# Loading x a second time in 32x32 blocks, so that VectorE and not TensorE turns it

## The chip, the cores and the metric

The kernel runs on one core of one Trainium2 chip. The metric is the device time of the whole program in microseconds; before the change it is 756.91 (median of 3 runs, 756.82 to 757.55). The engines are called as in the profile: PE is TensorE (PEld its weight loads), DVE is VectorE, ACT is ScalarE, POOL is GpSimd, SP is SyncE, which here only issues transfers.

## What is computed

There are 8 batches. In each, 8 heads hold 512 tokens of 64 numbers (x) and 32 state vectors of 64 numbers. Scores between the tokens and the states are normalised once over the states (for each token) and once over the tokens (for each state):

```python
scores = scale * x @ state.T              # B,H,512,32
a   = softmax(scores);  xread = a  @ state
a2  = softmax(scale * state @ x.T);  sread = a2 @ x
y = concatenate([xread, sread], axis=2)   # 544 rows in each batch
y = y.transpose(0, 2, 1, 3).reshape(B * 544, 512)
h = y @ w_in                              # 512 -> 2048
g = where(h > 0, h, exp(min(h, 0)) - 1)
out = g @ w_out                           # 2048 -> 512
```

All of it is in float32.

## The kernel before

**Tiling.** x of a batch lies in memory as x_sb with tokens on the 128 partitions (four tokens each, r = 0 to 3) and the 8 heads times 64 numbers along the row. The scores need it the other way round, with the 64 numbers of a head on partitions, two heads (one "m") in 128: this turned copy is called xT, four pieces of 128x512 in two tiles. The state vectors stand turned in kT. The scores of all 8 heads fill two banks of PSUM, each with 4 heads x 32 states on partitions and 512 tokens along the row.

**The attention's output is never written out.** make_m multiplies the state vectors by w_in to m (128x512, for each quarter c of the 2048 columns), so that ffn1, h = aT x m, goes straight from the normalised scores aT to the hidden layer: for each of 16 column blocks fo a product in two steps, in a bank of PSUM, then elu: two ScalarE operations and one VectorE operation that writes g_all. ffn1 uses three banks in turn.

**The second product** (g_all x w_out) is done by Strassen's scheme, in a class of that name: sums of parts of g_all are made on VectorE, and its seven partial products are queued as a list of steps. The first four steps are two pieces each of the products p1 and p2; from batch 2 on, four of the products are themselves done in this manner (class Second). After each step one of a list of hooks is called, and these hooks are the attention of the next batch:

- s0 turns x of the next batch: turn_x puts 32 TensorE transposes (64x64 each) into PSUM, copy_x copies the result in four ScalarE operations to xT. These two tiles come from the pool "o".
- s1 does the scores, make_m for the column quarters 0 and 1, and most of the softmax on VectorE, ScalarE and GpSimd.
- s2 turns the weights over tokens (turn_state), the last hook reads the state update (state_read, from x_sb) and keeps it.

**Order.** TensorE and SyncE follow the order in which the program names their instructions (class InOrder). ScalarE and GpSimd are held to it in the first batch only, VectorE until the end of batch 1's ffn1; after that a planner orders each engine's instructions by its estimates and their place in the program. The first batch has an order written out by hand and keeps its own turn of x for batches 0 and 1.

**Buffers and transfers.** Pool "o" has two buffers of 128x2x512 for all tiles with that tag: the two halves of a batch's output (o_sb) and, before the change, the two xT tiles. Pool "work" has 11 of the same size, six of which hold weight sums from batch 1 on. SyncE's queue holds, in each batch: the two stores of the previous output, the fetch of two w_in parts that had to give up their place (fetch_w_in, called at fo 6), a second such fetch together with s1, and the load of x_sb two batches ahead.

Of the kernel before, what the change touches and what calls it, by code (L numbers as in the profile page):

```python
# [10 lines left out]
FP32 = mybir.dt.float32  # L11
# [14 lines left out]
def kernel(  # L26
# [15 lines left out]
    B, H, S, D = x.shape  # L42
    NS = state.shape[2]
    DM, DF = moe_w_in.shape
    P = 128
    R = S // P
# [18 lines left out]
    def pool(name, bufs, **kw):  # L65
        return ctx.enter_context(tc.tile_pool(name=name, bufs=bufs, **kw))
# [6 lines left out]
    work = pool("work", NRAW + 4)  # L73
    small = pool("small", 4)
    epool = pool("elu", 3)
    opool = pool("o", 2)
# [8 lines left out]
    def bank(i):  # L85
        return psum[:, i]

    def pair(i):

        return psum[:, i : i + 2]  # L90
# [3 lines left out]
    class InOrder:  # L94
# [10 lines left out]
    tensor, sync, vector, scalar, gpsimd = (  # L105
        InOrder(e) for e in (nc.tensor, nc.sync, nc.vector, nc.scalar, nc.gpsimd)
    )
    matmul = tensor.matmul

    def transpose(out, in_):  # L110


        for t in range(2):
            rows = slice(t * 64, (t + 1) * 64)
            tensor.transpose(out[:, t], in_[rows], ident[rows, rows], tile_position=(t * 64, 0))
# [15 lines left out]
    x_t, st, m_t = {}, {}, {}  # L131

    def load_x(b, engines):
        x_t[b] = xpool.tile([P, R, DM], FP32, name="x_sb")
        x_v = x[b].rearrange("h (p r) d -> p r h d", r=R)
        for r in range(R):
            engines[r % len(engines)].dma_start(
                out=x_t[b][:, r].rearrange("p (h d) -> p h d", d=D), in_=x_v[:, r]
            )

    state_v = state.rearrange("b (m c) n d -> c m n b d", c=G)

# [82 lines left out]
    def turn_x(b, i, first=6):  # L225

        ps = pair(first).rearrange("p t (j r q) -> p t j r q", j=2, q=64)
        for j in range(2):
            for r in range(R):
                m = 2 * i + j  # L230
                transpose(ps[:, :, j, r], x_t[b][:, r, m * P : (m + 1) * P])
        st[b, "xT", i] = ps

    def copy_x(b, i):
        xT = opool.tile([P, 2, R * P], FP32, tag="o", name="xT")
        for j in range(2):
            st[b, 2 * i + j] = xT[:, j]
            scalar.copy(
                out=xT[:, j].rearrange("p (r t q) -> p t r q", t=2, q=64),
                in_=st[b, "xT", i][:, :, j],  # L240
            )
# [19 lines left out]
    def scores(b):  # L261

        st[b, "s_ps"] = by_state(b, [st[b, m][:, None] for m in range(NP)])
# [57 lines left out]
    def turn_state(b):  # L321
        ps = st[b, "sT"] = pair(6).rearrange("p g (r q) -> p g r q", r=R)
        for g in range(G):
            a = st[b, g, "a_s"].rearrange("p (r q) -> p r q", r=R)
            for r in range(R):
                tensor.transpose(ps[:, g, r], a[:, r], ident)

    def copy_state(b):
        st[b, "aT_s"] = work.tile([P, G, R, P], FP32, tag="w", name="aT_s")
        for g in range(G):  # L330
            scalar.copy(out=st[b, "aT_s"][:, g], in_=st[b, "sT"][:, g])

    def state_read(b):


        ps = st[b, "sr"] = pair(6)
        for g in range(G):
            for r in range(R):
                for m in range(NP):
                    matmul(  # L340
                        ps[m * NS : (m + 1) * NS, g, :D],
                        st[b, "aT_s"][:, g, r, m * NS : (m + 1) * NS],
                        x_t[b][:, r, m * P + g * D : m * P + (g + 1) * D],
                        start=(r == 0),
                        stop=(r == R - 1),
                        tile_position=(0, m * NS),
                    )

    def keep_read(b):
        for g in range(G):  # L350
            scalar.activation(
                out=read[:, b, g], in_=st[b, "sr"][:, g, :D], func=AF.Copy,
                scale=st[b, g, "total"],
            )
# [14 lines left out]
    def fetch_w_in(c, k):  # L369

        for i in range(2):
            sync.dma_start(
                out=w_in[:, 2 * (k + i) : 2 * (k + i) + 2],
                in_=w_in_mem[:, 2 * (c + i) : 2 * (c + i) + 2],
            )

    def make_m(b, c, h=None, first=6):

        c_in = c if b < 2 else c % 2
        halves = slice(2 * c_in, 2 * c_in + 2) if h is None else slice(2 * c_in + h, 2 * c_in + h + 1)  # L380
        assert h is None or b == 0
        st[b, "m", c] = by_state(b, [w_in[:, halves, m] for m in range(NP)], first)

    def copy_m(b, c, g, copy):
        if g == 0:
            m_t[b, c] = mpool.tile([P, G, 512], FP32, name="m_sb")
        copy(out=m_t[b, c][:, g], in_=st[b, "m", c][:, g])
# [8 lines left out]
    def exp_part(ps):  # L396
        e = epool.tile([P, ps.shape[-1]], FP32, tag="e", name="e_sb")
        scalar.activation(out=e, in_=ps, func=AF.Relu, scale=-1.0)
        scalar.activation(out=e, in_=e, func=AF.Exp, scale=-1.0)
        return e  # L400

    def max_part(fo, e, ps):
        vector.scalar_tensor_tensor(
            out=g_all[:, fo, : ps.shape[-1]], in0=e, scalar=-1.0, in1=ps,
            op0=ALU.add, op1=ALU.max,
        )

    def elu(ps, fo):

        max_part(fo, exp_part(ps), ps)  # L410

    def ffn1(b, fo):


        ps = bank(4 + fo % 2 if b == 0 else 3 + (fo + 1) % 3)
        for k in range(G):
            matmul(
                ps,
                m_t[b, fo // 4][:, k, fo % 4 * P : (fo % 4 + 1) * P],
                st[b, k, "aT"],  # L420
                start=(k == 0),
                stop=(k == G - 1),
            )
        return ps
# [243 lines left out]
    def attention(b):  # L668


        def both(*fs):
            for g in range(G):
                for f in fs:
                    f(b, g)

        def s0():

            for i in range(2):
                turn_x(b, i, 4 + 2 * i)
            for i in range(2):  # L680
                copy_x(b, i)

        def s1():

            scores(b)
            for c in range(2):
                make_m(b, c, first=4 - 2 * c)
            both(column_max, turn_scores, column_exp, row_max, row_subtract, row_exp)
            both(row_sum, row_scale, column_total)
            for c in range(2):  # L690
                for g in range(G):
                    copy_m(b, c, g, (scalar.copy, vector.tensor_copy)[g])

        def s2():
            turn_state(b)
            copy_state(b)
            both(turn_tokens)

        nop = lambda: None
        return [s0, s1, nop, nop, s2, lambda: (state_read(b), keep_read(b))]  # L700

    def store(b, i, o_sb):
        rows = out_b[b, 0:S].rearrange("(p r) c -> p r c", r=R)
        sync.dma_start(out=rows[:, 2 * i : 2 * i + 2], in_=o_sb)
# [107 lines left out]
            store(0, i, o_sb)  # L812

    def batch(b):
        for fo in range(FO):
            elu(ffn1(b, fo), fo)
            if fo == FO // 4 + 1:
                for c in (2, 3):
                    make_m(b, c, first=6 if c == 2 else 0)
            if FO // 4 + 1 <= fo < FO // 4 + 5:  # L820
                c, g = divmod(fo - FO // 4 - 1, G)
                copy_m(b, 2 + c, g, vector.tensor_copy)
            if b == 1 and fo % 2 == 1:
                weight_sum((1, 2, 4, 3)[fo // 4], fo % 4 // 2)
            if b > 1 and fo == FO // 4 + 2:
                fetch_w_in(0, 0)
        vector.on = False
        nxt = b + 1 < B
        hooks = attention(b + 1) if nxt else [turn_read]
        if nxt and b > 0:  # L830
            s1 = hooks[1]
            hooks[1] = lambda: (s1(), fetch_w_in(2, 0))
        if b + 2 < B:
            hooks += [lambda: load_x(b + 2, [sync])]
        if b == 1:
            hooks += [lambda: second[4].weights(t_w[4]), lambda: second[3].weights(b22)]
            hooks += [lambda: second[5].weights(t_w[1]), lambda: second[7].weights(t_w[3])]
            used = {k: second[k] for k in (4, 3)}
        else:
            used = second  # L840
        whole = Strassen(2, used)
        whole.sums()
        for f in whole.steps():
            f()
            if hooks:
                hooks.pop(0)()
        if not nxt:
            fetch_w_in(2, 2)
        for i in (1, 0):
            store(b, i, whole.o_sb[i])  # L850
# [61 lines left out]
```

## Time and profile before

The profile shows one execution, 756.0 us long. A batch in the middle, from one turn to the next, has these times (the batch that turns x of batch 4, from the timeline; the next batch starts 82.07 us later with the same steps):

| What | From us | Length us |
|---|---|---|
| ffn1, 16 column blocks, with make_m for quarters 2 and 3 between | 295.6 | 29.5 |
| first piece of p1 | 325.10 | 3.6 |
| turn of x (TensorE) | 328.65 | 1.2 |
| second piece of p1 | 329.80 | 3.7 |
| scores, make_m for quarters 0 and 1 | 333.45 | 2.7 |
| p2 | 336.18 | 7.2 |
| first piece of the third product | 343.19 | 3.6 |
| state read | 351.07 | 1.1 |
| last output store issued (of the batch before) | 296.1 | 2.7 to landing |
| w_in fetch, two transfers of 1 MB | 307.17 | to about 314 |

Groups that concern the change, from the answers on the tiles x_sb and xT:

| Operation | Count | Median ns |
|---|---|---|
| PE MATMUL ps<-ident,x_sb (turns of x; half of the records carry a form) | 256 | 223 |
| PE MATMUL ps<-xT,kT (scores) | 128 | 613 |
| ACT COPY xT<-ps | 32 | 591 |
| transfers x_sb<-in_x_dram, 256 KB each | 32 | 4.5 us to landing |

How to read it: records of TensorE overlap, so the length of a step is read from the start of one to the start of the next. A number in brackets at the end of a row of the timeline is the idle time of that engine ahead of the instruction, with what ended it. Every instruction of the kernel carries line 100, since a helper records them all; groups are told apart by the names of their tiles.

### The profile page before, as it was taken

How to read it: one execution, taken by the hardware profiler on the slowest of the kernel's cores; microseconds unless marked ns; L12 is line 12 of the kernel's file. 1: busy time of each engine (PE TensorE's matmuls, PEld its weight loads, DVE VectorE, ACT ScalarE, POOL GpSimd, SP SyncE). 2: the span in 40 equal slices, each digit the busy share in tenths (PEclk: the TensorE clock that was granted, in tenths of full speed). 3: DMA queues.
4: the chain of work that ended last, by engine and by line, in shares of the span. 5: the costliest groups of instructions: out<-in, count | busy, mean ns of one | idle time of the engine just before them, and what ended most of it. 6: DMA issues, size and time to landing. Idle time of an engine off the chain costs nothing.

```text
span 756.0 us, 11509 instructions
## 1 busy us (share of the span) xinstructions
PE 736.2 (97%) x4712; PEld 512.6 (68%) x4712; DVE 465.4 (62%) x856; ACT 312.0 (41%) x575; POOL 34.4 (5%) x38
## 2 busy tenths in 40 slices
PE   4899999999999999999999999999999999999997
PEld 2544344368955797468946795479846894699886
DVE  2999974899246673667455763667366755557330
ACT  5899955653036311642055303631164205510420
POOL 0200002002000200011000200020000100000000
PEclk9999999999999999999999999999999999999999
DMA  9667900403212331214030221233121103003000
GB/s 284 212 202 245 310 0 23 91 1 117 51 64 104 112 57 57 111 69 100 29 140 0 113 56 60 108 113 56 57 112 57 56 29 139 1 0 141 28 4 26
DMA packets 49566, 66.81 MB, mean 88 GB/s; under 512 B 36968, under 2 KB 37480, under 8 KB 45672
## 3 DMA queue, kind: packets, MB, share of 16 engines
q1 hardware_dynamic: 47204, 65.45, 26.3%
q10 hardware_dynamic: 2308, 0.62, 0.4%
q8 instruction: 37, 0.61, 0.4%
q14 instruction: 17, 0.14, 0.1%
HBM read 52.95 MB, written 13.11 MB: 87 GB/s over the span
## 4 chain that ended last, share of the span: by engine, by line
PE 93%; DVE 3%; DMA 1%; ACT 1%; ACTq 0%; issue 0%; DVEq 0%
PE ps L100 93%; DVE w_in L100 1%; DMA x_sb<-in_x_dram 1%; DVE s L100 0%; DMA raw<-in_moe_w_out_dram 0%; DVE w_out L100 0%; ACT xT L100 0%; DVE g_all L100 0%; ACTq L100 0%; DVE top L100 0%; ACT raw L100 0%; ACT a_s L100 0%; DVE t_sb L100 0%; ACT e_sb L100 0%; DVE aT L100 0%; DVE m_sb L100 0%
## 5 line engine op out<-in xcount | busy, mean ns | idle before, releaser
L100 PE MATMUL ps<-w_out,g_all 128*128 128x256 f32 (+2 forms) x1088 | 234.8, 367 | 1.5 <-DVE g_all L100 0.8
L100 PE MATMUL ps<-aT,m_sb 128*128 128x512 f32 x512 | 226.3, 595 | 1.1 <-DVE m_sb L100 0.8
L100 PEld LDWEIGHTS ps<-w_out,g_all 128*128 128x128 f32 x1088 | 175.6, 191 | 55.0 <-issue 37.1
L100 PEld LDWEIGHTS ps<-aT,m_sb 128*128 128x128 f32 x512 | 95.4, 190 | 122.0 <-issue 116.9
L100 ACT ACTIVATE e_sb<-ps 128x512 f32<-128x512 f32 (+1 forms) x144 | 82.5, 573 | 218.8 <-PE ps L100 203.5
L100 DVE SCALAR_TENSOR_TENSOR g_all<-e_sb,ps 128x512 f32<-128x512 f32 (+1 forms) x144 | 94.4, 657 | 112.5 <-ACT e_sb L100 112.4
L100 DVE TENSOR_TENSOR o_sb<-o_sb,ps 128x128 f32<-128x128 f32 (+2 forms) x170 | 52.8, 310 | 76.1 <-PE ps L100 74.4
L100 PE MATMUL ps<-t_w,s 128*128 128x256 f32 (+1 forms) x480 | 89.3, 338 | 0.0
L100 ACT ACTIVATE e_sb<-e_sb 128x512 f32<-128x512 f32 (+1 forms) x144 | 87.3, 606 | 4.6
L100 PEld LDWEIGHTS ps<-t_w,s 128*128 128x128 f32 x480 | 77.1, 191 | 7.3 <-DVE o_sb L100 0.2
L100 ACT COPY o_sb<-ps 128x512 f32<-128x512 f32 (+2 forms) x52 | 21.2, 424 | 122.2 <-PE ps L100 115.2
L100 ACT ACTIVATE raw<-raw 128x512 f32<-128x512 uint32 x64 | 43.8, 684 | 1.0
L100 POOL TENSOR_TENSOR t_sb<-t_sb,top_t 128x512 f32<-128x512 f32 x16 | 16.7, 1049 | 533.5 <-DVE top_t L100 533.5
L100 DVE TENSOR_TENSOR s<-s,g_all 128x512 f32<-128x512 f32 (+1 forms) x36 | 32.1, 896 | 14.4 <-PE ps L100 14.2
L100 DVE TENSOR_TENSOR g_all<-g_all,s 128x512 f32<-128x512 f32 (+1 forms) x36 | 31.9, 886 | 9.6 <-PE ps L100 9.6
L100 PE MATMUL ps<-w_in,kT 64*32 64x512 f32 (+1 forms) x576 | 33.2, 547 | 0.8 <-ACT a_s L100 0.8
L100 DVE TENSOR_TENSOR g_all<-g_all 128x512 f32<-128x512 f32 (+1 forms) x36 | 32.2, 895 | 0.5
L100 PE MATMUL ps<-t_w,g_all 128*128 128x128 f32 (+1 forms) x240 | 32.1, 282 | 0.0
L100 DVE TENSOR_TENSOR s<-g_all 128x512 f32<-128x512 f32 (+1 forms) x36 | 31.6, 895 | 0.5
L100 PE MATMUL ps<-w_in,s 128*128 128x128 f32 x240 | 30.7, 275 | 0.0
L100 PEld LDWEIGHTS ps<-t_w,g_all 128*128 128x128 f32 x240 | 29.8, 192 | 0.5
L100 PEld LDWEIGHTS ps<-w_in,s 128*128 128x128 f32 x240 | 28.7, 192 | 0.0
(82 smaller groups left out, 574.8 us busy)
## 6 DMA issues: line engine op xcount, KB each, us to landing
w_in<-w_in_mem SPq DMA_DIRECT2D x26, 1024.0 KB, 5.9
raw<-in_moe_w_in_dram SPq DMA_DIRECT2D x16, 512.0 KB, 4.9
raw<-in_moe_w_out_dram SPq DMA_DIRECT2D x16, 512.0 KB, 4.4
out_dram<-o_sb SPq DMA_DIRECT2D x16, 512.0 KB, 2.6
x_sb<-in_x_dram SPq DMA_DIRECT2D x30, 256.0 KB, 4.5
w_in_mem<-w_in SPq DMA_DIRECT2D x4, 1024.0 KB, 8.6
x_sb<-in_x_dram ACTq DMA_DIRECT2D x2, 256.0 KB, 6.7
s_sb<-in_state_dram SPq DMA_DIRECT2D x8, 56.0 KB, 2.0
```

Source lines behind the costliest of these rows:

```text
L100: ins = getattr(self.engine, name)(*args, **kw)
```

## The change

x of batches 2 to 7 is loaded a second time. load_blocks, called at the start of the batch before, fetches it in pieces of 32 tokens by 32 numbers (128 bytes in a row), each placed where its turned counterpart belongs; what remains is to turn the inside of every 32x32 block. VectorE does so: turn_blocks, one 128x512 piece at each of fo 12 to 15. The raw blocks lie in pool "o" (before the output of that batch takes it), the turned ones in pool "work". TensorE's transposes and ScalarE's copies of these batches go, and with them s0; s1 moves up to the first hook, one piece of the product sooner, with a nop in its old place. It is meant to take the turn off TensorE. x_sb is still loaded, since state_read uses it.

```diff
+    def load_blocks(b):
+        for i in range(2):
+            st[b, "blocks", i] = raw = opool.tile([P, 2, R * P], FP32, tag="o", name="x_blocks")
+            for j in range(2):
+                for k in range(4):
+                    x_v = x[b, 2 * (2 * i + j) + k // 2].rearrange(
+                        "(q p r) d -> p r q d", q=P // 32, r=R
+                    )
+                    sync.dma_start(
+                        out=raw[k * 32 : (k + 1) * 32, j].rearrange(
+                            "p (r q d) -> p r q d", r=R, d=32
+                        ),
+                        in_=x_v[:, :, :, k % 2 * 32 : (k % 2 + 1) * 32],
+                    )
+
+    def turn_blocks(b, m):
+        i, j = divmod(m, 2)
+        if j == 0:
+            st[b, "xT", i] = work.tile([P, 2, R * P], FP32, tag="w", name="xT_b")
+        st[b, m] = st[b, "xT", i][:, j]
+        vector.transpose(st[b, m], st[b, "blocks", i][:, j])
...
-        def s0():
-            for i in range(2):
-                turn_x(b, i, 4 + 2 * i)
-            for i in range(2):
-                copy_x(b, i)
...
-        return [s0, s1, nop, nop, s2, lambda: (state_read(b), keep_read(b))]
+        return [s1, nop, nop, nop, s2, lambda: (state_read(b), keep_read(b))]
...
     def batch(b):
+        if b + 1 < B:
+            load_blocks(b + 1)
         for fo in range(FO):
             elu(ffn1(b, fo), fo)
+            if fo > 11 and b + 1 < B:
+                turn_blocks(b + 1, fo - 12)
...
-            s1 = hooks[1]
-            hooks[1] = lambda: (s1(), fetch_w_in(2, 0))
+            s1 = hooks[0]
+            hooks[0] = lambda: (s1(), fetch_w_in(2, 0))
```

## The prediction, as put on record before the result was known

> **What bounds the kernel now.** I read the busy times first, then the chain of waits in order of time, then the timeline of one middle batch. From the page:
>
> ```profile
> PE 736.2 (97%) x4712; PEld 512.6 (68%) x4712; DVE 465.4 (62%) x856; ACT 312.0 (41%) x575; POOL 34.4 (5%) x38
> PE 93%; DVE 3%; DMA 1%; ACT 1%; ACTq 0%; issue 0%; DVEq 0%
> ```
>
> TensorE (PE) is busy 97% of the span, and the chain that ended last is 93% TensorE. In order of time, its later part repeats (start, length, what):
>
> ```profile
> 273.12 81.05 PE ps L100 x560
> 354.17 0.04 DVEq L100
> 354.20 0.73 DVE s L100 x2
> 354.94 0.21 DVE o_sb L100
> 355.14 0.04 issue
> 355.19 81.05 PE ps L100 x560
> ```
>
> A batch lasts 82.07 us (355.19 less 273.12), 81.05 of them unbroken TensorE work. So in the middle batches, a microsecond taken out of TensorE's queue comes off the total, and one added to another engine costs nothing until TensorE waits for it. The timeline where the first Strassen product of batch 3 begins, while x of batch 4 is turned (start, length, engine, operation):
>
> ```profile
> 325.10 3.62 PE L100 MATMUL ps<-w_out,g_all 128*128 128x256 f32 x16
> ...
> 328.65 1.22 PE L100 MATMUL ps<-ident,x_sb 64*128 64x64 f32 x32
> ...
> 329.40 2.05 ACT L100 COPY xT<-ps 128x512 f32<-128x512 f32 x4 [2.84 <-PE ps L100]
> ...
> 329.80 3.72 PE L100 MATMUL ps<-w_out,g_all 128*128 128x256 f32 x16
> ...
> 333.45 1.09 PE L100 MATMUL ps<-xT,kT 64*32 64x512 f32 x16
> ...
> 336.18 7.17 PE L100 MATMUL ps<-w_out,g_all 128*128 128x256 f32 x32
> ```
>
> TensorE goes from one piece of the product to the 32 transposes, to the next piece, to the scores, with no idle time noted: starts follow one another. The four ScalarE copies run beside the second piece, so they are off the path.
>
> **What the skill says.** "VectorE: DVE Perf Modes", section "The three transpose paths": VectorE transposes only within 32x32 blocks, so blocks must be placed by something else; here the loads do it. The trace shows that operation at 0.71 us for 128x512 out of on-chip memory (line below). "DMA: Bandwidth & Descriptors", section "Specifications", names 512 B as the least size for full rate; the trace agrees: the 256 B pieces of x move at 216 to 289 GB/s, the 4 KB rows of the output at 401. The same page, "Why small descriptors are slow (HBM only)", gives a piece 3 cycles above its 32-byte beats: 11 for 256 B, hence 7 for 128 B. No run here shows 128 B pieces yet.
>
> **Removed from TensorE and ScalarE.** The turn stands from 328.65 to the next piece at 329.80: 1.15 us, on the path. Moving the scores forward one piece changes order, not work. From 325.10 to 336.18 there are 11.08 us; without the turn I count two pieces of 16 x 0.2235 (the spacing that 3.576 us for 16 gives), 7.15, and scores with make_m, 336.18 less 333.45, 2.73, and about 0.08 for changing to the tiled form, as between the second piece and the scores now: 9.96. That gives 1.12, near the 1.15. I take 1.13. Batches 1 to 6 do this for the next one: 6 x 1.13 = 6.8 us. Four ScalarE copies per batch (median 0.59 us) go too, at nothing gained, since the pieces hide them.
>
> **Added to VectorE.** Four block transposes per batch; the nearest row has the same shape:
>
> ```profile
> 342.38 0.71 DVE L100 STREAM_TRANSPOSE aT<-t_sb 128x512 f32<-128x512 f32 x1 [0.56 <-POOL t_sb L100]
> ```
>
> In ffn1, VectorE does one 0.69 us operation every 1.72 us and sits idle 1.03 us before it:
>
> ```profile
> 321.44 0.69 DVE L100 SCALAR_TENSOR_TENSOR g_all<-e_sb,ps 128x512 f32<-128x512 f32 x1 [1.03 <-ACT e_sb L100]
> ...
> 323.16 0.69 DVE L100 SCALAR_TENSOR_TENSOR g_all<-e_sb,ps 128x512 f32<-128x512 f32 x1 [1.03 <-ACT e_sb L100]
> ```
>
> Counting back from the last at 326.74, these belong to fo 12 and 13. A 0.71 us transpose fits into each gap, so 4 x 0.71 = 2.84 us per batch lie beside matmuls: cost nothing. The last, behind fo 15's elu (326.74 + 0.69), would end about 328.1, with scores due at 328.7. Batch 1 is tighter: VectorE runs almost without gaps from 149 to 169 us, as it also makes weight sums there. Turn 3 then follows the elu that ends at 162.2; with one 1.22 us sum ahead of it, it ends at 164.1, against scores due at 163.6. I charge 0 to 1 us once, and take 0.2.
>
> **Added to the loads.** 16 transfers per batch, each 32 partitions x 16 pieces of 128 B: 8192 pieces, 512 on each of 16 DMA engines, 1 MB. The nearest rows are those of the normal load of x (4096 pieces of 256 B), half-microsecond windows with clock, DMA share and GB/s:
>
> ```profile
> 354.00:354.50 0.50, 1.00 1.27 289
> 354.50:355.00 0.50, 1.00 1.19 267
> 355.00:355.50 0.50, 1.00 1.22 238
> 355.50:356.00 0.50, 1.00 1.31 228
> ```
>
> The eight windows from 354 to 358 average 240 GB/s, that is 256 B x 16 / 240 = 17 ns per piece on one engine. A 128 B piece costs, at best, 7/11 of that (the page's beats): 10.9 ns, 5.6 us per batch; at worst I allow twice the 256 B price, 34 ns, 17.4 us. I take the same 17 ns, 8.7 us. The transfers need the two o buffers, free once the output of the batch before has been stored; the second store is issued at 296.1 and its bytes end at about 298.4. So data from 298.4, the first tile complete half way at 302.8 and the second at 307.1, plus 1.9 us (the normal load's bulk ends at 358.0, its last landing at 354.1 + 5.8): 304.7 and 309.0. Behind them on SyncE's queue stands the w_in fetch, issued at 307.17 now and finished near 314; delayed to about 316, it still meets make_m at 329. In program order the first turn is due at 322.1: 17 us to spare, and 8 at the worst price. Cost: nothing.
>
> **Added waits.** A turn waits on a transfer; behind it on VectorE stand the elu of following fo, on which ffn1's three banks hang. This is where it can fail: only in batch 1's ffn1 is VectorE held to program order. Afterwards its order is the planner's, which puts an instruction into the first gap where it believes the data there (a 1.22 us sum for the product already stands at 311.87, between two elus). If it believes that the blocks land sooner than they do, VectorE stands still. The buffers for the turned x (work pool) are free during ffn1; the previous product's sums are done.
>
> Sum: 756.91 - 6.8 + 0.2 = 750.3 us.
>
> **Rivals.**
> (A) All hidden, 750.3. For it: the gaps and the spare time above.
> (B) Turns placed too early by a few microseconds. Say the planner puts them behind elus 1 to 4, 301 to 306 us. At 17 ns, the turns wait until 304.7 and 309.0. TensorE fills its banks first, about 3.4 us beyond the delayed elu, so of 3 to 4 us delay 0 to 2 reach it, also through the m_sb copies of 0.68 us behind. A loss of 1 us in five batches eats most of the gain: about 755.5; 2 us give 760.
> (C) The same with 34 ns pieces: landings near 309 and 318. Elu 2 would end near 310, where TensorE wanted its bank at 304.2: 5 to 6 us lost, and nearly as much again at the second tile: 10 us x 5 = 50 at the extreme, 800. If only one tile's wait hits, 5 x 5 = 25: 775. Slower. Against: the programmed place has 8 us to spare even then.
> (D) The last turn stands behind the product's sums (1.22 at 325.60, then 1.83, 0.69, 0.69 up to 330.6): scores wait for it until 331.3, 2.6 us after 328.7, a loss of 1.5 per batch after the gain: 5 x 1.5 = 7.5, 764. Against: the turn is ready long before the sums and comes earlier in the program.
>
> **How the numbers follow.** A 0.60, B 0.15, C 0.18, D 0.07. Predicted is A, 750.3. The range starts at 749.2 (1.15 per batch and no charge, with 0.8 for a measurement and small waits that vanish) and reaches to 770, taking in B, D and the lower part of C; about 0.12 of C lies above and 0.03 below the range. Faster by over 0.2% (below 755.4): A and half of B, 0.67. Within: 0.06. Slower (above 758.4): C, most of D, the rest of B: 0.27.
>
> **What would show it.** Right: no TensorE rows with ident and x_sb after batch 1; scores follow the first piece directly; the batch lasts 80.9 us; transposes named xT_b at about 0.7 us in gaps of ffn1, with no VectorE idle time released by a DMA; data of the blocks moving at about 120 GB/s for 8 to 9 us from about 298. Wrong: VectorE idle "<-DMA x_blocks", TensorE idle in ffn1 released by g_all or m_sb; scores idle "<-DVE xT_b"; or the blocks' transfers taking 16 us and more.

## The result

753.01 us (median of 4 runs, 751.73 to 754.15) against 757.23 before (4 runs): a ratio of 0.9943, 95% interval 0.9922 to 0.9964. The change gains 4.2 us, where 6.6 were forecast. The four runs lie in two pairs, near 752 and near 754 us, which the last experiment takes up.

The page of the changed kernel, busy times and the chain's shares by engine:

```profile
PE 730.9 (97%) x4520; PEld 507.0 (67%) x4520; DVE 479.5 (64%) x880; ACT 299.5 (40%) x551; POOL 34.6 (5%) x38
PE 90%; DVE 6%; DMA 1%; ACT 1%; issue 1%; SPq 0%; DVEq 0%; ACTq 0%
```

TensorE has 192 records and 5.3 us less, VectorE 24 instructions and 14 us more, ScalarE 24 copies less. The chain in order of time, from the middle of batch 1 on (start, length, what):

```profile
166.46 104.44 PE ps L100 x612
...
274.93 76.69 PE ps L100 x448
351.64 1.24 DVE s L100
352.93 0.57 issue
353.51 1.17 DVE s L100 x2
354.71 0.68 DVE s L100
355.40 0.21 DVE o_sb L100
355.65 76.69 PE ps L100 x448
```

A middle batch now lasts 80.72 us (355.65 less 274.93), 1.35 less than the 82.07 of before. The chain goes over VectorE's sums for some 4 us, yet TensorE works on meanwhile (busy for 3.96 of the 4.10 us from 351.6 on, as in the same stretch before); it is only the chain's path that changed. The timeline of TensorE in the same batch shows what was wanted: no turn, and the scores behind the first piece.

```profile
326.91 3.62 PE L100 MATMUL ps<-w_out,g_all 128*128 128x256 f32 x16
330.46 1.09 PE L100 MATMUL ps<-xT_b,kT 64*32 64x512 f32 x16
331.34 1.92 PE L100 MATMUL ps<-w_in,kT 64*32 64x512 f32 x32
333.19 10.63 PE L100 MATMUL ps<-w_out,g_all 128*128 128x256 f32 x48
343.66 1.67 PE L100 MATMUL ps<-t_w,s 128*128 128x256 f32 x7
```

But the point that read 273.12 before reads 274.93 now, 1.81 us later, although the gain of two turns, those of batches 2 and 3, already lies ahead of it. Something in batch 1 costs more than those two give. The kernel before begins p1 of batch 1 at 160.07:

```profile
160.07 3.62 PE L100 MATMUL ps<-w_out,g_all 128*128 128x256 f32 x16
```

The changed kernel comes to this point 0.55 us sooner, so the loss lies behind it. Its timeline of TensorE there:

```profile
159.52 3.62 PE L100 MATMUL ps<-w_out,g_all 128*128 128x256 f32 x16
163.06 1.08 PE L100 MATMUL ps<-xT_b,kT 64*32 64x512 f32 x12
166.46 0.62 PE L100 MATMUL ps<-xT_b,kT 64*32 64x512 f32 x2 [2.32 <-DVE xT_b L100]
...
166.93 4.00 PE L100 MATMUL ps<-w_in,kT 64*32 64x512 f32 x26
170.86 10.63 PE L100 MATMUL ps<-w_out,g_all 128*128 128x256 f32 x48
```

Three quarters of the scores run (12 of 16 matmuls), then TensorE waits for the last of the four turned tiles. Scores and make_m, 2.73 us in a middle batch (330.46 to 333.19), take 7.80 here (163.06 to 170.86): 5.07 lost. Why the tile is late stands in VectorE's timeline:

```profile
160.51 0.70 DVE L100 STREAM_TRANSPOSE xT_b<-x_blocks 128x512 f32<-128x512 f32 x1
161.13 0.65 DVE L100 SCALAR_TENSOR_TENSOR g_all<-e_sb,ps 128x512 f32<-128x512 f32 x1
161.71 1.21 DVE L100 TENSOR_TENSOR g_all<-g_all 128x1024 f32<-128x1024 f32 x1
162.84 2.35 DVE L100 TENSOR_TENSOR s<-g_all 128x1024 f32<-128x1024 f32 x2
165.10 0.69 DVE L100 TENSOR_TENSOR t<-t_w,t 128x512 f32<-128x512 f32 x1
165.70 0.70 DVE L100 STREAM_TRANSPOSE xT_b<-x_blocks 128x512 f32<-128x512 f32 x1
```

Between the elu of fo 15 (161.13) and the last turn (165.70) stand four sums that TensorE does not need yet. No row has idle time ahead of it: VectorE did not wait for the transfer, it worked on other things first. And the wait has a tail: make_m needs 4.00 us and not 1.92, since TensorE's clock was halved. Windows of 1 us (length, TensorE busy, count, clock, DMA share, GB/s):

```profile
166.00:167.00 1.00, 0.54 (x16) 1.00 0.00 0
167.00:168.00 1.00, 1.00 (x24) 0.50 0.00 0
168.00:169.00 1.00, 1.00 (x16) 0.50 0.00 0
169.00:170.00 1.00, 1.00 (x10) 0.50 0.08 16
170.00:171.00 1.00, 1.00 (x5) 0.80 0.62 98
```

Half speed for three windows and 0.8 in a fourth loses 1.7 us of the 5.07. The other 3.4 us are the wait; its idle time is noted as 2.32 us at the row of the matmul and as 3.23 at that of the weight load.

### The profile page after: what moved, and what is told of

It reads as the page before. It is cut to its first block, busy times and chain, and to the rows that moved or that the text cites. A ratio compares the mean times of both kernels' runs of the same rounds, so it can differ in the third digit from the quotient of the medians.

```text
span 752.0 us, 11295 instructions
## 1 busy us (share of the span) xinstructions
PE 730.9 (97%) x4520; PEld 507.0 (67%) x4520; DVE 479.5 (64%) x880; ACT 299.5 (40%) x551; POOL 34.6 (5%) x38
## 4 chain that ended last, share of the span: by engine, by line
PE 90%; DVE 6%; DMA 1%; ACT 1%; issue 1%; SPq 0%; DVEq 0%; ACTq 0%
PE ps L100 90%; DVE s L100 2%; DVE w_in L100 1%; DMA x_sb<-in_x_dram 1%; DVE g_all L100 1%; DMA raw<-in_moe_w_out_dram 0%; DVE w_out L100 0%; ACT e_sb L100 0%; ACT xT L100 0%; DVE xT_b L100 0%; DVE top L100 0%; ACT raw L100 0%; ACT a_s L100 0%; SPq L100 0%; DVE t_sb L100 0%
## 5 line engine op out<-in xcount | busy, mean ns | idle before, releaser
L100 PE MATMUL ps<-w_in,kT 64*32 64x512 f32 (+1 forms) x576 | 35.7, 567 | 1.8 <-ACT a_s L100 1.8
L100 ACT COPY aT_s<-ps 128x512 f32<-128x512 f32 x16 | 8.6, 586 | 54.1 <-PE ps L100 54.1
```

Of the source, the lines that this page charges most:

```text
L100: ins = getattr(self.engine, name)(*args, **kw)
```

## The experiments

The theory to test: the middle batches give all that they can, and what is missing from the sum is the place of one turn in VectorE's order in batch 1, with the clock behind it. Against it: the scores' earlier place makes part of the gain (R1), VectorE is too full in batch 1 wherever the turns stand (R2), or transfers and turns cost a little everywhere (R3).

**Scores back in their old place** (of the changed kernel, with the blocks and turns kept):

```diff
-        return [s1, nop, nop, nop, s2, lambda: (state_read(b), keep_read(b))]
+        return [nop, s1, nop, nop, s2, lambda: (state_read(b), keep_read(b))]
...
-            s1 = hooks[0]
-            hooks[0] = lambda: (s1(), fetch_w_in(2, 0))
+            s1 = hooks[1]
+            hooks[1] = lambda: (s1(), fetch_w_in(2, 0))
```

> The blocks and the VectorE turns stay; the scores go back to their old place, behind the second piece of p1. Theory T (the gain is short by what batch 1 loses: there the last of the four turns stands on VectorE behind five other operations, ends at 166.4 us, and TensorE, due at the scores at about 164.0, stands idle 2.3 us and then runs for some us at half clock; the middle batches gain 1.35 us each): with the second piece in between, the scores are due at about 166.6, so no idle time over 0.3 us in batch 1, middle batches still 80.7 us, total 756.9 - 6 x 1.35 = 748.8 (748.4 to 749.6). Rival R1 (part of the middle batches' gain comes from the scores being sooner): middle batches 80.9 to 82, total 750 to 754. Rival R2 (batch 1 loses because VectorE has four more operations in a full stretch, wherever they stand): total stays at 752 to 754.

Measured: 749.46 us (748.83 to 749.63, 4 runs), ratio to before 0.9883 (0.9867 to 0.9899). TensorE in batch 1, same view:

```profile
159.59 7.07 PE L100 MATMUL ps<-w_out,g_all 128*128 128x256 f32 x32
166.59 1.09 PE L100 MATMUL ps<-xT_b,kT 64*32 64x512 f32 x16
167.47 1.92 PE L100 MATMUL ps<-w_in,kT 64*32 64x512 f32 x32
```

The last turn still stands behind the same four sums and ends at 166.5 (165.78 + 0.70), but with another piece ahead of the scores, TensorE arrives at 166.59. No wait, no slow clock, and the middle batch lasts 80.72 us, the same to the hundredth. R1 falls: moving the scores sooner is worth nothing as long as no turn on TensorE stands between, and it is what exposed the late turn. (The expectation counts five operations ahead of the turn; four of them are sums, the first is the elu of fo 15.)

**Batch 2 turned in the old way**, by TensorE, and no blocks loaded for it (s0 is back for this one batch, and the second w_in fetch goes with s1 to its old place there; these lines are left out):

```diff
...
+        if b == 2:
+            return [s0, s1, nop, nop, s2, lambda: (state_read(b), keep_read(b))]
...
-        if b + 1 < B:
+        if 1 < b and b + 1 < B:
             load_blocks(b + 1)
...
-            if fo > 11 and b + 1 < B:
+            if fo > 11 and 1 < b and b + 1 < B:
```

> As the changed kernel, but x of batch 2 is turned by TensorE in the old way, with no blocks loaded for it in batch 1. T: batch 1 as before the change, batches 2 to 6 gain 1.35 us each: 756.9 - 6.75 = 750.2 (749.8 to 750.8), with no dip of the TensorE clock after 100 us. If the loss of the changed kernel were spread over all batches (rival R3: the transfers or the turns cost a little everywhere, hidden in the sum), the total would be 751.5 to 753.

Measured: 750.05 us (749.84 to 751.70, 5 runs), ratio 0.9896 (0.9879 to 0.9914). With one turn less taken off TensorE it is 3 to 4 us faster than the changed kernel (753.01 and, in its second series, 753.89): batch 2's share of the change was a loss. R3 would have put the total at 751.5 to 753; the median is below that, one run of the five (751.70) is not. The clock shows no slow stretch between 28.4 us and the end of the span.

**Blocks ahead of x_sb on SyncE's queue**, in batch 1 alone:

```diff
     first_batch()
+    load_blocks(2)
     load_x(2, [sync])
...
-        if b + 1 < B:
+        if 1 < b and b + 1 < B:
             load_blocks(b + 1)
```

> As the changed kernel, but the 16 block transfers for batch 2 stand on SyncE's queue ahead of the 4 transfers of x_sb for batch 2 and not behind them. T, with the cause of the late place: the planner takes the blocks to land later than they do, and its order puts the last turn of batch 1 where it believes the data there; 4 transfers fewer ahead of them move the last turn to directly behind the elu of fo 15. Then TensorE waits at most 0.5 us for it, and the total is 748.8 (748.4 to 749.8). R2 (four more operations on a full VectorE): 752 to 754. If the wait is for the data itself and not for VectorE's order, the turn ends no sooner than about 20 us after the first issue at 136, which is 156: no wait either, so this run does not tell that apart; the trace of the changed kernel does.

Measured: 749.05 us (748.46 to 749.69, 4 runs), ratio 0.9879 (0.9863 to 0.9896); the fastest version with the full computation, together with the first experiment, from which it can't be told apart. VectorE in batch 1, then TensorE:

```profile
162.07 0.65 DVE L100 SCALAR_TENSOR_TENSOR g_all<-e_sb,ps 128x512 f32<-128x512 f32 x1
162.64 0.69 DVE L100 STREAM_TRANSPOSE xT_b<-x_blocks 128x512 f32<-128x512 f32 x1
163.26 1.18 DVE L100 TENSOR_TENSOR w_out<-w_out 128x1024 f32<-128x1024 f32 x1
164.36 1.21 DVE L100 TENSOR_TENSOR g_all<-g_all 128x1024 f32<-128x1024 f32 x1
165.49 2.35 DVE L100 TENSOR_TENSOR s<-g_all 128x1024 f32<-128x1024 f32 x2
```

```profile
164.00 1.09 PE L100 MATMUL ps<-xT_b,kT 64*32 64x512 f32 x16
164.88 1.92 PE L100 MATMUL ps<-w_in,kT 64*32 64x512 f32 x32
166.73 10.63 PE L100 MATMUL ps<-w_out,g_all 128*128 128x256 f32 x48
```

The last turn now follows the elu directly, ends at 163.3, and TensorE finds it ready at 164.0: 2.73 us, as in a middle batch. VectorE does the same work as in the changed kernel, in another order, so R2 falls. Four transfers fewer ahead of the blocks changed the order; the data itself had long been there. In the changed kernel the 16 block transfers for batch 2 are issued from 135.66 to 148.0 and no transfer of this tile took more than 4.5 us to land, so all is there by 152.5, 13 us ahead of the late turn. It fits that the planner takes these transfers to be slower than they are; its estimates themselves were not looked at, so this reason for the late place is not shown.

**No turn inside the blocks** (the scores read raw blocks, so that part of the computation is left out):

```diff
-        if j == 0:
-            st[b, "xT", i] = work.tile([P, 2, R * P], FP32, tag="w", name="xT_b")
-        st[b, m] = st[b, "xT", i][:, j]
-        vector.transpose(st[b, m], st[b, "blocks", i][:, j])
+        st[b, m] = st[b, "blocks", i][:, j]
```

> As the changed kernel, but the VectorE turns inside the blocks are left out: the scores read the raw blocks. This takes all of VectorE's added work and the scores' wait for it away. T: 756.9 - 6 x 1.35 = 748.8 (748.4 to 749.4), the same as with the turns well placed: in the middle batches the 4 x 0.70 us on VectorE are hidden altogether (middle batch 80.7). R3 (the turns cost the middle batches something): middle batch below 80.6, total below 748.2. R2 is not told apart from T here.

Measured: 748.68 us (748.42 to 749.09, 4 runs), ratio 0.9875 (0.9859 to 0.9891), middle batch 80.72. It overlaps the previous experiment's range: well placed, 24 turns on VectorE cost nothing that can be seen. (In this kernel the scores do not wait for a turn at all.)

**Added only**: the kernel before with load_blocks and turn_blocks called in the same places, and the scores reading TensorE's xT as before (the added lines of the diff, but without setting st[b, m], and without any removed line).

> The kernel before, with all that the change adds and nothing that it removes: the block transfers and the VectorE turns run in the same places, but the scores still read the x that TensorE turned. T (the added work is hidden, and only TensorE's wait for the last turn of batch 1 costs): as before, 756.9 (756.6 to 757.6), middle batches 82.07 us. R2/R3 (the 8192 small pieces or the four turns cost a batch something by themselves): 758 to 761.

Measured: 757.02 us (756.54 to 758.40, 12 runs) against 757.34, ratio 0.9995 (0.9987 to 1.0004). Its chain:

```profile
354.57 78.03 PE ps L100 x480
436.64 78.03 PE ps L100 x480
```

82.07 us (436.64 less 354.57), as before. Six times 8192 small pieces and 24 turns are hidden whole. R3 falls.

**Sooner, with the old turn** (the kernel before, no blocks; the second w_in fetch moves with s1, lines left out):

```diff
-        return [s0, s1, nop, nop, s2, lambda: (state_read(b), keep_read(b))]
+        return [lambda: (s0(), s1()), nop, nop, nop, s2, lambda: (state_read(b), keep_read(b))]
...
```

> The kernel before, with no blocks and no VectorE turns, but with the scores one piece sooner: directly behind TensorE's own turn of x. What the earlier scores are worth by themselves: one interruption of the product fewer saves about 0.2 us per batch, but the scores must wait for ScalarE's four copies of 0.5 us, which the second piece hides in the kernel before; they end at 331.45 where TensorE is free at 329.8. T: middle batches 82.07 - 0.2 + 1.3 to 1.7 = 83.2 to 83.6, total 756.9 + 6 x 1.3 = 764.7 (763 to 767). If an idle time of 1.5 us already lowers TensorE's clock as the 2.3 us of the changed kernel did, about 2 us more in those batches: up to 777. If the earlier scores were what gave the gain: below 756.

Measured: 766.62 us (765.91 to 766.95, 4 runs), ratio 1.0115 (1.0102 to 1.0128). TensorE in a middle batch, and the chain:

```profile
331.69 1.22 PE L100 MATMUL ps<-ident,x_sb 64*128 64x64 f32 x32
334.56 1.09 PE L100 MATMUL ps<-xT,kT 64*32 64x512 f32 x16 [1.64 <-ACT xT L100]
335.44 1.93 PE L100 MATMUL ps<-w_in,kT 64*32 64x512 f32 x32
337.30 10.63 PE L100 MATMUL ps<-w_out,g_all 128*128 128x256 f32 x48
```

```profile
276.17 56.26 PE ps L100 x328
359.76 56.26 PE ps L100 x328
```

The second piece of p1 was what hid ScalarE's copies; without it TensorE waits 1.64 us in each of six batches. The clock stayed at 1.00 through all six of these waits, from 28.5 us to the end of the span, whereas the longer wait of the changed kernel was followed by half clock. From the turn to the scores there are 2.87 us, 1.72 more than the turn alone takes in the kernel before, yet the batch lasts 83.59 us, only 1.52 more: the other 0.2 us are the interruption saved.

**The changed kernel again**, beside these:

> The changed kernel once more, beside the others on one chip. T: without the dip of the TensorE clock behind the 2.3 us of idle time in batch 1, 756.9 - 8.1 + 2.3 = 751.1; with it (3.4 us at half clock, 1.7 to 2.2 us lost), about 753.2. So runs should fall into two groups near 751.5 and 753.8, mean granted clock about 1.0 and 0.995, and none near 749.

Measured: 753.89 us (751.58 to 754.57, 6 runs), ratio 0.9945 (0.9933 to 0.9957). One time lies at 751.58, with a mean clock of 0.999; the other five lie from 753.7 to 754.57, four of them at 0.995 and one at 0.998. The four times of the result fall apart in the same way: 751.73 and 752.19 at 1.000 and 0.999, 753.83 and 754.15 at 0.995. None is near 749.

This profile too has the wait of 2.32 us, and half clock for 3.41 us from 167.1 on. Both profiles of the changed kernel belong to the upper group. Both have a second such stretch in the first batch, near 24 us; the profiles of three other versions (batch 2 in the old way, no turn, sooner) have that early one alone, at a mean clock of 0.998. So 0.995 stands for two stretches, and the run at 753.86 and 0.998 fits one, that of batch 1. The early one is no rival for the 2 us between the groups, since it hardly shows in the time: "added only" takes 756.8 to 757.3 us in its runs at a clock of 1.000 and 757.0 to 757.8 in those at 0.997 and 0.998 (its one run at 0.995, so with two stretches, takes 758.4).

The Trainium skill, "TensorE: Matmul & The Clock Gate", section "What's actually happening", says that the clock is set by how busy TensorE was in a window of about 3.4 us that runs freely. The traces agree: in both profiles a slow stretch lasts 3.41 us, the full speed between the two lasts 139.95 us, 41 times as much, and the wait lies whole in the 3.41 us before the slow stretch (in the first profile idle from 164.1 to 166.5, slow from 167.0). In the lower group the wait may have been split over two windows; no profile caught one, so that is not shown.

## Why the prediction was right, and where it was off

- **What bounds the kernel**: right. TensorE's queue alone sets a middle batch, and what the change took from it came off each of them in full.
- **Removed from TensorE**: right in kind, too small. 1.13 us was forecast per batch, 1.35 measured. The term that was mis-sized is the step from the product to the tiled form and back. The four pieces of p1 and p2 take 14.21 us before (3.55 + 3.65 + 7.01, with the turn and the scores taken out; the third product starts at 343.19), 14.02 after (3.55 + 10.47, to 343.66). One interruption fewer saves 0.2 us on top of the 1.15 of the turn. The working left 0.08 for the interruption that stays and took 3.576 us for each of two pieces, where they take 3.55 and 3.49 (a third of 10.47) now. The Trainium skill, "TensorEngine Tiling (Array Packing)", section "Key Properties", says that changing the tiling mode drains TensorE; the 0.2 us fit, though no run measures a drain by itself.
- **Added to VectorE**: right. 0.70 us each, and hidden (757.02 and 748.68 above).
- **Loads**: hidden, as forecast. The block windows from 300 to 310.5 us show 64 to 142 GB/s, for 1 MB in about 10.5 us, hence 20 ns per piece on one engine, where 17 was taken and 10.9 was the best case: half the bytes did not make a piece cheaper here. In the changed kernel's timeline of SyncE the issues themselves fill that time, 16 in 10.87 us, with the DMA engines busy 0.4 to 0.9:

```profile
298.34 10.87 SPq L100 DMA_DIRECT2D x_blocks<-in_x_dram  x16
309.31 24.40 SPq L100 DMA_DIRECT2D w_in<-w_in_mem  x4
```

- **Added waits and rivals B and C**: no turn waited for a transfer. The planner put the turns of a middle batch at 308.05, 312.16, 318.71 and 323.86, the last some 12 us after the last block had landed (issued by 309.2, 2.4 us to landing): late rather than early, and still in time for the scores at 330.46.
- **Batch 1, charged 0.2 us**: this step failed. It took VectorE to be held to program order there and let one sum stand ahead of the last turn; four did, 4.0 us of them. The order holds only among instructions that are named while it is switched on. These four sums are named after it is switched off, so the planner was free to put them ahead. This is rival D's mechanism, in the one batch where VectorE is full and the x_sb load stands directly ahead of the blocks, and the sign named for it, scores idle "<-DVE xT_b", appears there once. What was held against D, that the turn is ready long before the sums and comes earlier in the program, was true and did not help. The step also put no price on the half clock that can follow an idle TensorE. Its true size is 5.07 us in place of 0.2: so much by the timeline, and so much by the times, as the changed kernel gains 3.45 us on the kernel before beside it (757.34 less 753.89) and the one with the blocks first 8.52 (757.57 less 749.05).

The two errors have opposite signs, 6 x 0.22 = 1.3 us more gain and up to 4.9 more loss. The gain forecast was 6.6 us, the gain measured 4.2, and 3.45 in the second series. That the total came out only 2.7 us from the forecast is in part luck, as the larger gain covers some of the loss. With the first correction alone the forecast would have been 749.0, near the 749.46 and 749.05 that two of the experiments measure.

## What to carry to other kernels

Work moved off the bounding engine is worth its length plus the interruption it made, as long as its new place is ready in time in every stage; the one stage with a full helper engine can give back more than half. When a planner orders an engine, look at where each new instruction stands and not only at whether there is room for it; here, moving transfers ahead on their queue was enough to put the order right. And do not move a consumer sooner than its new producer allows: the earlier place gained nothing here and cost 4 to 5 us.

## What the runs showed that was not expected

- A wait of 2.3 us (3.2 by the weight load) was followed by 3.4 us at half clock in two profiles of two; six waits of 1.64 us were followed by none. By their times and clocks, about three of the ten runs of the changed kernel escaped the slow stretch.
- Pieces of 128 B, 512 to a transfer, cost 0.68 us of issue for a transfer (10.87 / 16) and landed in 2.4 us (median). The issues stand back to back while the DMA engines are 0.4 to 0.9 busy, so it seems that they set the pace of about 100 GB/s; no run varied the issue alone.
